# Reordering the head of a fused DeltaNet and SwiGLU kernel: chunk 1's gate/value products ahead of chunk 0's outputs, weight conversions in pairs, the first M turned by TensorE

## The chip, the cores and the metric

One Trainium2 chip, one core of it. The metric is the device time of one launch in microseconds (us), the median of several executions. The core's engines are TensorE (PE in the profile, with its weight loads as PEld), VectorE (DVE), ScalarE (ACT), GpSimd (POOL) and SyncE (SP, which here only issues transfers). They run their own programs and wait for one another at semaphores. In the profiles a record is one logged operation; a float32 product leaves two on TensorE here. The granted clock is the share of TensorE's full clock (1.00) that was let through. "Issue" marks a wait whose cause the profile doesn't show.

## The reference

The reference draws the three weight matrices as float64, and the kernel gets them as 64-bit words.

```python
# q, k, v: (4, 8, 768, 48); beta: (4, 8, 768); w_gate, w_val: (384, 1536); w_out: (1536, 384)
k_n = k / (np.linalg.norm(k, axis=-1, keepdims=True) + 1e-06)
for t in range(S):                       # the delta rule, one (48, 48) state per head
    kt, vt, bt = (k_n[:, :, t], v[:, :, t], beta[:, :, t, None])
    y[:, :, t] = np.einsum('bhd,bhde->bhe', q[:, :, t], state)
    v_old = np.einsum('bhde,bhd->bhe', state, kt)
    state = state + bt[:, :, :, None] * np.einsum('bhd,bhe->bhde', kt, vt - v_old)
x = y.transpose(0, 2, 1, 3).reshape(B * S, H * D)        # 3072 tokens of 384
g = x @ w_gate
return ((g / (1 + np.exp(-g))) * (x @ w_val)) @ w_out
```

The kernel cuts the sequence into 12 chunks of 64 steps (256 tokens each). A chunk needs the inverse of a triangular matrix per head; two chunks share one inversion, which is done by substitution in blocks of 32 on VectorE and then joined by small products on TensorE. Three sets of products of a chunk's recurrence follow (`p_u`, `p_s`, `p_y`), and their result `x_ffn` goes through the SwiGLU part: 6 groups of gate and value products, then 2 sets of output products.

Names in the profiles: `p_...` are TensorE's results, before another engine copies them out. `kn` are the normalized keys, `kt` and `qt` the transposed keys and queries, `p_g` their Gram products (all pairs within a chunk), `a_sb` the copied Gram matrix, M the scaled blocks of it that substitution inverts, `zt` the inverse (its buffer first stages weights), `uu` the copied `p_u`, `h_f` silu(gate) times value. To turn a matrix is to transpose it.

## The kernel before

The weights arrive as float64 and are made into float32 on the chip, in 30 pieces: 18 of 512 columns for gate and value, 12 of 384 for the output weights. VectorE takes the words apart in five steps and ScalarE rebuilds the exponent between the first and the fourth:

```python
def convert(*ns):
    ...
    # VectorE: power <- words & 0x7FF00000; ScalarE: power <- rebias(power)
    # VectorE: mant  <- words & 0xFFFFF | 1<<20
    # VectorE: mant  <- low word * 2**-32 + mant
    # VectorE: power <- sign | power
    # VectorE: dst   <- mant * 2**-20 * power
    for n in ns:
        stage(n + DEPTH)          # four staging places, one transfer each
```

The pieces stand between the groups of chunk 0. The pace holds back: eight output pieces are left for the last groups. Then come chunk 0's outputs:

```python
def fill(c, at):
    if c == 0 and todo:
        n = len(filled)
        filled.append(n)
        due = len(pieces) - len(todo)
        upto = min((n // 4 + 2) * 2 * KT, N_WO)
        for _ in range(max(-(-(upto - due) // (4 - n % 4)), n // 8)):
            converts(1)
        while n == FT - 1 and todo:
            converts(2)
...
def ffn(c, point, fill):
    for f in range(0, FT, 2):
        point(c)                  # a step of the next chunk's recurrence or preparation
        ...                       # gate products, silu, value products, h_f, with fill(...)
    for bp in range(NB):
        point(c)
        ...                       # 12 output products, copy, store
...
gram(0, False); gram(1, False, "py")
turned(0, True); turned(1, True)
for _ in invert(0):               # turn M (VectorE), scale, 31 substitution steps, turn back
    pass
gram(0, True)
one = join(0, slice(0, 1))
...                               # join and recurrence of chunk 0, one piece beside each step
for c in range(NCH):
    ffn(c, point, fill)
    ...
```

Of the kernel before, what the change touches and what calls it, by code (L numbers as in the profile page):

```python
# [21 lines left out]
def kernel(  # L22
# [120 lines left out]
    DEPTH = 4  # L143
    staged = {}
    wo_flat = wo_sb.bitcast(U32).rearrange("p t d -> p (t d)")
    zt_flat = ztp[1].bitcast(U32).rearrange("p c h i -> p (c h i)")
    N_WO = len(pieces) - FT * (DM // m_wo)

    def stage(n):
        if n >= len(pieces):  # L150
            return
        _, src, t, f0, m = pieces[n]
        if n < N_WO:
            place = wo_flat[:, n % DEPTH * 2 * PIECE :][:, 0 : 2 * m]
        elif n % DEPTH < 2:
            place = zt_flat[:, n % DEPTH * 2 * PIECE :][:, 0 : 2 * m]
        else:
            tag = ("mb", "zb")[n % DEPTH - 2]
            place = work.tile([128, 2 * PIECE], U32, name="staged", tag=tag, bufs=1)
            place = place[:, 0 : 2 * m]  # L160
        staged[n] = place.rearrange("p (f two) -> p f two", two=2)
        nc.sync.dma_start(
            out=place, in_=src[t * 128 : (t + 1) * 128, f0 : f0 + m].bitcast(U32)
        )

    def convert(*ns):

        work_of = []
        for n in ns:
            dst, _, t, f0, m = pieces[n]  # L170
            words = staged.pop(n)
            mant, power = (
                ffn_pool.tile([128, PIECE], U32, name=name, tag="sil", bufs=4)[:, 0:m]
                for name in ("mant", "power")
            )
            work_of.append((dst[:, t, f0 : f0 + m], words, mant, power))
        for _, words, _, power in work_of:
            nc.vector.tensor_scalar(  # L178
                out=power,
                in0=words[:, :, 1],  # L180
                scalar1=0x7FF00000,
                scalar2=None,
                op0=ALU.bitwise_and,
            )

            nc.scalar.activation(  # L186
                power.bitcast(I32), power, ACTF.Relu, bias=rebias, scale=8.0
            )
        for _, words, mant, _ in work_of:
            nc.vector.tensor_scalar(  # L190
                out=mant,
# [6 lines left out]
        for _, words, mant, _ in work_of:  # L198
            nc.vector.scalar_tensor_tensor(  # L199
                out=mant.bitcast(FP32),  # L200
                in0=words[:, :, 0],
                scalar=2.0**-32,
                in1=mant,
# [3 lines left out]
        for _, words, _, power in work_of:  # L207
# [8 lines left out]
        for dst, _, mant, power in work_of:  # L216
            nc.vector.scalar_tensor_tensor(  # L217
                out=dst,
                in0=mant.bitcast(FP32),
# [5 lines left out]
        for n in ns:  # L225
            stage(n + DEPTH)
# [10 lines left out]

    mask_k = const.tile([128, C], FP32, name="mask_k")
    mask_q = const.tile([128, C], FP32, name="mask_q")
    for m in (mask_k, mask_q):  # L240
        nc.gpsimd.memset(m, 1.0)
        for b in range(2):
            rows = m[64 * b : 64 * b + 64]
            nc.gpsimd.affine_select(
                out=rows,
                in_=rows,
                compare_op=ALU.is_ge,
                fill=0.0,
                base=-1,
                pattern=[[1, C]],  # L250
                channel_multiplier=-1,
            )
    for b in range(2):
        nc.gpsimd.memset(mask_k[64 * b : 64 * b + R, R:C], 0.0)
        nc.gpsimd.memset(mask_k[64 * b + R : 64 * b + C, 0:R], -1.0)
# [71 lines left out]

    def turned(c, of_q, tag=None):

        x = qpad[c % QB] if of_q else knp[c % AHEAD]  # L330
        xt = work.tile([128, NB, NJ, 2, C], FP32, name="qt" if of_q else "kt", bufs=AHEAD)
        (qt if of_q else kt)[c] = xt
        p_t = ps_pair("p_t", tag or ("py" if of_q else "px")).rearrange("p bp (j n) -> p bp j n", j=NJ)
        for bp in range(NB):
            for j in range(NJ):
                nc.tensor.transpose(p_t[:, bp, j], x[:, bp, 2 * j : 2 * j + 2], ident)  # L336
        nc.scalar.copy(xt.rearrange("p bp j b i -> p bp j (b i)"), p_t)  # L337
# [3 lines left out]
    def gram(c, of_q, tag=None):  # L341

        xt = (qt if of_q else kt)[c]
        p_g = ps_pair("p_g", tag or ("py" if of_q else "px")).rearrange("p par (bp j i) -> p par bp j i", bp=NB, j=NJ)
        for bp, j, par, b, _ in every():
            nc.tensor.matmul(  # L346
                p_g[half_of(b if of_q else b ^ par), par, bp, j],
# [3 lines left out]
        if of_q:  # L351
            p_sb[c] = work.tile([128, 2, NB, NJ, C], FP32, name="p_sb", bufs=AHEAD)
            dst = p_sb[c].rearrange("p par bp j i -> p (par bp j) i")
        else:
            g = c // 2
            if c % 2 == 0:
                a_sb[g] = work.tile([128, 2, HH, C], FP32, name="a_sb")
            dst = a_sb[g][:, c % 2]
        nc.vector.tensor_tensor(  # L359
            out=dst,  # L360
            in0=p_g.rearrange("p par bp j i -> p (par bp j) i"),
            in1=(mask_q if of_q else mask_k)[:, None, :].to_broadcast([128, HH, C]),
            op=ALU.mult,
        )
# [12 lines left out]
    def invert(g):  # L377
# [9 lines left out]
        a_v = a_sb[g].rearrange("p c h i -> p i (c h)")  # L387
        z_v = ztp[g % ZB].rearrange("p c h i -> p i (c h)")
        yield from turn(
            lambda rows, half: mb[rows].rearrange("p j i -> p i j"),  # L390
# [418 lines left out]
```

## Time and profile before

| | before |
|---|---|
| device time, median of 4 runs beside the changed kernel | 816.22 us (813.55 to 816.87) |
| profiled span | 816.2 us |
| TensorE, VectorE, ScalarE, GpSimd busy | 88%, 53%, 18%, 10% |
| start to first gate product | 83.4 us, VectorE busy 66.3 |
| first gate product to end of conversions | 75.0 us, VectorE busy 69.8 |
| end of conversions to end of chunk 1's outputs | 76.6 us, TensorE busy 75.1 |
| hand-over to chunk 2 | 17.8 us |
| chunks 2 to 11 | 563.4 us, TensorE busy 559.2 |

The averages mislead: 559 of TensorE's 720 busy us lie in the last stage. The first 252.8 us are called the head below. The lines behind this table stand in the prediction.

### The profile page before, as it was taken

What the parts mean: (1) busy time and instruction counts of PE and PEld (TensorE: products, weight loads), DVE (VectorE), ACT (ScalarE), POOL (GpSimd) and SP (SyncE); (2) the same over time, 40 slices, a digit from 0 to 9 for tenths busy, and PEclk for the clock granted to TensorE, in tenths of its full rate; (3) what the DMA queues carried; (4) which work ended last, traced back from release to release, by engine and by line L of the source; (5) the groups of instructions that cost most, each with busy time, mean ns of one, the idle gap of its engine ahead of it and who ended that gap; (6) DMA issues with size and microseconds to landing.
All of it is one profiled execution on the core that took longest, in us unless ns stands there. A gap on an engine that the chain in (4) does not pass through costs nothing.

```text
span 816.2 us, 20536 instructions
## 1 busy us (share of the span) xinstructions
PE 719.5 (88%) x9384; PEld 573.6 (70%) x9384; DVE 430.8 (53%) x768; ACT 145.0 (18%) x230; POOL 80.5 (10%) x73
## 2 busy tenths in 40 slices
PE   3304868399989999999999999999999999999997
PEld 2303757268758877868868868868868778688784
DVE  3899799849824785207881157852277511011010
ACT  2003223311012111121201211211202111021110
POOL 6000032122003020030110121100000000000000
PEclk9655899599998999999999999999999999999999
DMA  8604564412013120120210211001001000000000
GB/s 192 110 1 105 174 174 110 132 31 50 0 25 58 22 49 12 22 49 15 44 23 12 40 31 31 2 21 22 2 20 22 2 21 2 10 12 1 19 1 19
DMA packets 85094, 34.45 MB, mean 42 GB/s; under 512 B 78064, under 2 KB 81136, under 8 KB 85008
## 3 DMA queue, kind: packets, MB, share of 16 engines
q1 hardware_dynamic: 79008, 27.93, 14.9%
q10 hardware_dynamic: 6000, 5.21, 2.7%
q8 instruction: 73, 1.20, 0.6%
q14 instruction: 13, 0.11, 0.0%
HBM read 28.41 MB, written 4.72 MB: 41 GB/s over the span
## 4 chain that ended last, share of the span: by engine, by line
PE 77%; DVE 15%; issue 4%; DMA 2%; POOL 1%; ACT 1%; ACTq 0%; POOLq 0%; DVEq 0%
PE p_gate L574 22%; PE p_o L595 21%; PE p_val L574 21%; PE p_g L346 2%; PE p_t L336 2%; DVE mant L199 2%; DVE power L208 2%; DVE zb L410 1%; DVE tmp L404 1%; PE p_u L505 1%; PE p_y L535 1%; DVE mant L190 1%; PE p_s L522 1%; PE p_r L484 1%; PE p_y L493 1%
## 5 line engine op out<-in xcount | busy, mean ns | idle before, releaser
L574 PE MATMUL p_gate<-x_ffn,wg_sb 128*128 128x256 f32 x864 | 205.7, 388 | 0.0
L574 PE MATMUL p_val<-x_ffn,wv_sb 128*128 128x256 f32 x864 | 198.7, 379 | 0.5 <-DVE wv_sb L217 0.5
L595 PE MATMUL p_o<-wo_sb,h_f 128*128 128x384 f32 x576 | 191.1, 490 | 0.0
L574 PEld LDWEIGHTS p_val<-x_ffn,wv_sb 128*128 128x128 f32 x864 | 164.0, 190 | 23.4 <-DVE wv_sb L217 1.2
L574 PEld LDWEIGHTS p_gate<-x_ffn,wg_sb 128*128 128x128 f32 x864 | 161.6, 192 | 23.6 <-DVE wg_sb L217 0.5
L587 DVE TENSOR_TENSOR h_f<-sil,p_val 128x512 f32<-128x512 f32 x72 | 49.3, 685 | 226.7 <-PE p_val L574 226.6
L595 PEld LDWEIGHTS p_o<-wo_sb,h_f 128*128 128x128 f32 x576 | 108.9, 191 | 72.7 <-issue 0.9
L583 ACT ACTIVATE sil<-p_gate 128x512 f32<-128x512 f32 x72 | 43.0, 597 | 211.2 <-PE p_gate L574 192.0
L410 DVE TENSOR_TENSOR zb<-zb,tmp 128x31 f32<-128x31 f32 (+15 forms) x186 | 68.5, 368 | 6.4
L404 DVE TENSOR_TENSOR tmp<-zb,mb 128x31 f32<-128x31 f32 (+15 forms) x186 | 67.8, 364 | 5.0
L314 POOL TENSOR_TENSOR norm<-norm,half 128x16 f32<-128x16 f32 x12 | 35.4, 2953 | 165.4 <-DVE norm L308 163.6
L603 ACT COPY o_sb<-p_o 128x384 f32<-128x384 f32 x24 | 11.5, 480 | 202.7 <-PE p_o L595 202.7
L318 POOL TENSOR_TENSOR kn<-kin,norm 128x768 f32<-128x768 f32 x10 | 14.8, 1479 | 293.6 <-DVE norm L317 246.6
L359 DVE TENSOR_TENSOR a_sb<-p_g,mask_k 128x1024 f32<-128x1024 f32 x12 | 14.7, 1223 | 45.2 <-PE p_g L346 45.2
L346 PE MATMUL p_g<-kt 64*64 64x64 f32 x768 | 16.1, 244 | 19.1 <-ACT kt L337 19.1
L446 PE MATMUL p_j<-zt,a_sb 32*32 32x32 f32 x768 | 8.3, 197 | 26.2 <-DVE zt L369 26.2
L346 PEld LDWEIGHTS p_g<-kt 64*64 64x64 f32 x768 | 14.5, 156 | 23.2 <-ACT kt L337 19.6
L186 ACT ACTIVATE power<-power,rebias 128x512 int32<-128x512 uint32 (+1 forms) x30 | 19.9, 677 | 58.4 <-DVE power L178 56.2
L446 PEld LDWEIGHTS p_j<-zt,a_sb 32*32 32x32 f32 x768 | 7.5, 108 | 28.8 <-issue 28.7
L372 DVE STREAM_TRANSPOSE zt<-zb 32x1024 f32<-32x1024 f32 x12 | 26.3, 2188 | 0.1
L372 DVE STREAM_TRANSPOSE mb<-a_sb 32x1024 f32<-32x1024 f32 x12 | 25.6, 2136 | 0.3
L465 DVE COPY zt<-p_j 32x1024 f32<-32x1024 f32 (+1 forms) x7 | 7.5, 1070 | 32.3 <-ACT zt L465 32.2
(85 smaller groups left out, 548.1 us busy)
## 6 DMA issues: line engine op xcount, KB each, us to landing
wo_sb<-in_moe_w_gate_dram SPq DMA_DIRECT2D x9, 512.0 KB, 3.6
wo_sb<-in_moe_w_val_dram SPq DMA_DIRECT2D x9, 512.0 KB, 3.8
qpad<-in_q_dram SPq DMA_DIRECT2D x48, 96.0 KB, 3.0
vin<-in_v_dram SPq DMA_DIRECT2D x96, 48.0 KB, 2.4
out_dram<-o_sb ACTq DMA_DIRECT2D x48, 96.0 KB, 2.2
kin<-in_k_dram SPq DMA_DIRECT2D x44, 96.0 KB, 2.9
staged<-in_moe_w_out_dram SPq DMA_DIRECT2D x6, 384.0 KB, 3.2
zt<-in_moe_w_out_dram SPq DMA_DIRECT2D x6, 384.0 KB, 3.6
```

What stands on the lines that cost most here:

```text
L186: nc.scalar.activation(power.bitcast(I32), power, ACTF.Relu, bias=rebias, scale=8.0)
L199: nc.vector.scalar_tensor_tensor(out=mant.bitcast(FP32), in0=words[:, :, 0], scalar=2.0**-32, in1=mant, op0=ALU.mult, op1=ALU.add,)
L208: nc.vector.scalar_tensor_tensor(out=power, in0=words[:, :, 1], scalar=0x80000000, in1=power, op0=ALU.bitwise_and, op1=ALU.bitwise_or,)
L314: nc.gpsimd.tensor_tensor(out=norm, in0=norm, in1=half, op=ALU.pow)
L346: nc.tensor.matmul(p_g[half_of(b if of_q else b ^ par), par, bp, j], kt[c][half_of(par), bp, j, b], xt[half_of(par), bp, j, b],)
L372: nc.vector.transpose(out(rows, 0), in_(rows, 0))
L404: nc.vector.tensor_tensor(out=t_v, in0=zb[:, 0 : j + 1, j : j + 1].to_broadcast([128, j + 1, m]), in1=mb[:, j : j + 1, j + 1 : R].to_broad ...
L410: nc.vector.tensor_tensor(out=zb[:, 0 : j + 1, j + 1 : R], in0=zb[:, 0 : j + 1, j + 1 : R], in1=t_v, op=ALU.add,)
L574: nc.tensor.matmul(ps[name][:, i], w_sb[:, t, (f + i) * 128 : (f + i + 1) * 128], x[:, t], start=(t == 0), stop=(t == KT - 1),)
L583: nc.scalar.activation(sil, ps[name], ACTF.Silu)
L587: nc.vector.tensor_tensor(out=hs[-1][:, f % 4 : f % 4 + 2], in0=sil, in1=ps["p_val"], op=ALU.mult)
L595: nc.tensor.matmul(p_o, hs[f // 4][:, f % 4, bp * 128 : (bp + 1) * 128], wo_sb[:, f], start=(f == 0), stop=(f == FT - 1),)
```

## The change

Its intent is to let TensorE work through the conversions: chunk 1's gate/value products need no output weights, so four of chunk 1's six groups go ahead of chunk 0's outputs. VectorE's chain is shortened: pieces go in pairs (a step of one hides the latency of the other's), the exponent is asked for a pair ahead, eight pieces are staged early, and the first M is turned by 128 small products instead of three VectorE transposes. The diff, cut to its core:

```diff
 def convert(ns, ahead=2):
     ...                                  # pairs; mantissas are built in dst itself
+        for n in range(ns[-1] + 1, ns[-1] + 1 + ahead):
+            power_step(n)                # exponents of the next pair
     ...
 def fill(n):
     if todo:
+        converts(2 - len(filled) % 2)    # 2, 1, 2, 1, ...
+        filled.append(n)
-        ...                              # the old pace
+def invert_first(g, between):
+    for j in range(R):
+        for quad, at in QUADS:
+            nc.tensor.matmul(
+                p_m[quad, R * j : R * j + R], a_v[quad, :, at + j], ident[quad, quad])
+    between(0)                           # four exponents, two pieces
+    scale_m(mb, p_m.rearrange("p (j i) -> p j i", i=R), nbeta)
+    between(1)                           # query transposes and Gram products
+    for _ in substitute(mb, zb):
+        pass
+    ...
+def join_first(g, c, tags):
+    # first set: 32 products 32x32, two ScalarE copies; second set: 32 of 32x64, two copies
 ...
-        for c in range(NCH):
-            ffn(c, point, fill)
+        second = join_first(0, 1, ("px", "py"))       # chunk 1's join: before the first group
+        for f in range(0, FT, 2):
+            point(1)
+            gate_val(0, f, fill)
+        finish(1)
+        for f in range(0, FT, 2):
+            if f == 8:
+                while todo:
+                    converts(2)
+                for bp in range(NB):
+                    point(2)
+                    output(0, bp, fill)
+            point(2)
+            gate_val(1, f, fill)
+        for bp in range(NB):
+            point(2)
+            output(1, bp, fill)
```

## The prediction

> **What bounds the kernel now.** I read three views. First, the busy time per engine, cut at five moments that I chose after looking at the timeline: the first gate product (83.4), the end of the weight conversions (158.4), the end of chunk 1's outputs (235.0), the first gate product of chunk 2 (252.8), the end.
>
> ```profile
> core 0: us, PE busy (x) PEld busy (x) DVE busy (x) ACT busy (x) POOL busy (x), PEclk, DMA share, GB/s
> 0.00:83.40 83.40, 24.90 (x775) 22.05 (x775) 66.26 (x123) 14.73 (x24) 13.96 (x28) 0.68 0.48 108
> 83.40:158.40 75.00, 48.16 (x613) 40.69 (x612) 69.76 (x137) 23.86 (x38) 11.52 (x6) 0.82 0.52 152
> 158.40:235.00 76.60, 75.06 (x736) 56.37 (x732) 52.28 (x91) 9.46 (x14) 12.54 (x9) 0.97 0.12 25
> 235.00:252.80 17.80, 12.16 (x472) 11.27 (x472) 4.42 (x6) 5.37 (x8) 5.08 (x3) 0.81 0.25 48
> 252.80:816.20 563.40, 559.17 (x6806) 443.25 (x6805) 238.07 (x412) 91.62 (x147) 37.43 (x29) 1.00 0.10 20
> ```
>
> From 252.8 on TensorE is busy 559.2 of 563.4 us at full clock: only less TensorE work would shorten that part, and the change removes none there. The head, 252.8 us, is the target. Up to 158.4 VectorE is the bound (66.3 of 83.4 us, then 69.8 of 75.0); TensorE idles 58.5 + 26.8 us there. From 158.4 to 235 TensorE is full again.
>
> Second, TensorE's timeline where the two bounds meet, and the hand-over to chunk 2:
>
> ```profile
> 134.32 2.75 PE L574 MATMUL p_val<-x_ffn,wv_sb 128*128 128x256 f32 x12
> 136.91 1.04 PE L336 MATMUL p_t<-ident,kn 128*128 128x128 f32 x8
> 137.78 1.04 PE L336 MATMUL p_t<-ident,qpad 128*128 128x128 f32 x8
> 156.84 1.99 PE L346 MATMUL p_g<-kt 64*64 64x64 f32 x64 [18.02 <-ACT kt L337]
> 158.60 1.93 PE L346 MATMUL p_g<-qt,kt 64*64 64x64 f32 x64
> 160.46 9.17 PE L595 MATMUL p_o<-wo_sb,h_f 128*128 128x384 f32 x24
> ```
>
> Chunk 0's gate/value products end at 137, but TensorE stands still for 18.0 us until ScalarE has copied kt. That copy stands in ScalarE's program behind the exponent steps of the last eight pieces, which wait for VectorE. In truth this is a wait for the output weights: chunk 0's outputs come next and need all 30 pieces. Chunk 1's products, which need none of the output weights, only begin at 182.
>
> Third, VectorE's timeline, for the price of a piece. A lone gate piece, then a pair of output pieces:
>
> ```profile
> 119.72 0.69 DVE L217 SCALAR_TENSOR_TENSOR wg_sb<-mant,power 128x512 f32<-128x512 f32 x1
> 120.33 0.42 DVE L178 TENSOR_SCALAR power<-wo_sb 128x512 uint32<-128x512 uint32 x1
> 120.66 0.42 DVE L190 TENSOR_SCALAR mant<-wo_sb 128x512 uint32<-128x512 uint32 x1
> 121.12 0.69 DVE L199 SCALAR_TENSOR_TENSOR mant<-wo_sb,mant 128x512 f32<-128x512 uint32 x1
> 121.73 0.68 DVE L208 SCALAR_TENSOR_TENSOR power<-wo_sb,power 128x512 uint32<-128x512 uint32 x1
> 122.44 0.69 DVE L217 SCALAR_TENSOR_TENSOR wv_sb<-mant,power 128x512 f32<-128x512 f32 x1
> ...
> 142.72 0.62 DVE L178 TENSOR_SCALAR power<-staged 128x384 uint32<-128x384 uint32 x2
> ...
> 146.61 0.62 DVE L178 TENSOR_SCALAR power<-zt 128x384 uint32<-128x384 uint32 x2
> ```
>
> Starts are what counts: 120.33 to 123.05 (the next piece) is 2.72 us for a lone piece of 512, with starts 0.33, 0.46, 0.61, 0.71, 0.61 apart. The steps that need the one just before (0.46, 0.71) lose 0.10 to 0.13. A pair has other work in between: 142.72 to 146.61 is 3.89 us for two pieces of 384, or 1.95 each. For a pair of 512 I estimate 2 x (0.33 + 0.33 + 3 x 0.61) = 4.98.
>
> **What the skill says.** "TensorE: Matmul & The Clock Gate", section What's actually happening: the array's clock is halved until TensorE has been busy for some 3.4 us. The trace agrees: the granted clock was 0.50 from 40 to 60 us, and the first twelve gate products took 5.01 us against 2.75 to 2.86 later. "GPSIMD Engine Reference", section Specifications: GpSimd shares its memory interfaces with VectorE instructions that take two inputs or use both ports. It shows: while GpSimd scaled a kn (109.35 to 110.87) and squared the next, two conversion steps took 1.69 and 1.83 instead of 0.42 and 0.69. "Perfetto Trace Analysis", section Optimization Strategy, advises interleaving regimes with different bounds: that is this change.
>
> **The change, part by part.** The program order of every engine can be read from the built kernels, so I walked the head by hand with durations of this trace.
>
> 1. Start to the first gate product. Norm 1 now stands behind norm 0's power step (2.93 us on GpSimd): kn of chunk 1 comes at 18.3, not 17.2. The second Gram matrix ends at 24.0 and goes out through ScalarE (two copies, about 1.1). The three VectorE transposes (24.26 to 30.70, 6.4 us) go; instead 128 small products, 256 records. Those of beta took 1.50 us for 96, so 4.0. Scaling M starts at 29.3 instead of 30.8: only 1.5 gained on the path, but VectorE uses the wait for four exponent masks and two pieces (5.7 us). Substitution is unchanged (23.4 us), ending at 53.9. Then one full transpose (2.2) and one into d_t (2.1) replace three (6.4) and the six of z1 (2.3), and the mask of p_g leaves the path: first join products at 56.1, two ScalarE copies of 0.57, second products about 1.4, two copies of 1.0: p_u at 61.9, against 68.9. Of these 7.0 us I give back about 4: uu, y and x_ffn stand on ScalarE behind exponent steps of pieces 4 to 10, which VectorE reaches only at 64 to 77; and the second half of the join stands before the first gate product. Gate product: about 80 instead of 83.4, with nine pieces done or nearly so instead of six.
>
> 2. Conversions. From 78 on: pieces 9, 10 (5.0), then idle until the slow-clock value product at 87.6 for h_f (4.4 lost). After h_f, at 88.3: pieces 11 to 17 (3 lone x 2.72 + 2 pairs x 4.98 = 18.1), 18 to 28 (3 lone x 2.1 + 4 pairs x 3.9 = 21.9), five more h_f (0.6 each, 3.0), two masks, two reductions, r, state, small norm steps (about 5.7), GpSimd collisions (twice 2.4): 53.5 in all, to 141.8. Then h_f of chunk 1's first group and piece 29: 144.4. Staging output weights goes round four places only, and the exponent wants its words a pair ahead, with some 2.7 us between the freeing and the need, against 3.2 to 3.6 from issue to landing: 2 to 3 us more. End at 146.5 instead of 158.4: 11.9 gained.
>
> 3. What TensorE has left then. Before: two p_g, four outputs, six groups, five more products and transposes, 76.6. After: chunk 0's six groups and chunk 1's first are done; its second ends near 149.5, and four groups (5.2 each, 20.8), four outputs (4 x 7.8 = 31.2) and four small ones (about 3.7) follow: outputs end at 205.2, 58.7 after the conversions. 17.9 gained. VectorE's second inversion begins when chunk 3's Gram matrix is out (about 158) and is spread over the same groups. Its last steps come behind h_f of the last group (190): nine substitution steps 5.2, three transposes 6.5, z1 2.3: 204. It just fits.
>
> 4. Hand-over to chunk 2: 17.8 before. One join product set (1.3) and its copy (0.6) no longer lie beside the last output, so 19.4: 1.6 lost. First gate product of chunk 2: 224.6 instead of 252.8, 28.2 earlier.
>
> 5. The rest. From there both orders agree row by row, but the query side is done just in time: two chunks' query transposes and Gram products (0.87 + 1.01 each) move from the head into the full part: 3.8 lost.
>
> Sum: 11.9 + 17.9 - 1.6 - 3.8 = 24.4; 815.7 - 24.4 = 791.3. Say 791.
>
> **Rivals.** (a) VectorE and TensorE wait for each other in chunk 0's groups: each h_f stands between a pair and a lone piece, h_f waits for TensorE, TensorE for PSUM or for uu behind exponent steps (5.7 us before, 5.3 in my walk). I found one VectorE wait of 4.4; for it speaks the shorter order with three pieces per group from the first, against it that VectorE needs about 8 us per group and TensorE about 6.5. If there were three such waits: some 8 us lost, 799. (b) The second inversion ends the head: it fits by 1 us in my walk. Every GpSimd collision or late Gram copy goes straight into the hand-over; 5 to 8 us, 797 to 799. (c) The output weights' transfers end the conversions: before, DMA ran at about half its time here without stalling VectorE, but the exponents now need words earlier. One us per piece would be 10: 801. (d) Better than I think: the Gram copies in halves and the deeper early staging bring VectorE's idle to nothing and ScalarE's queue is short: 783.
>
> **Range and chances.** The tail (563 us) is safe to within 2 us, so all doubt is in the head. Two rivals at half strength give 799, the good case 783. Range 783 to 800. Two per cent is 799.4: faster 0.87, within 2% 0.12, slower 0.01.
>
> **What would show it.** In the changed profile: p_m of 256 records in about 4 us; no 18 us wait for kt; last conversion near 146; outputs of chunk 0 after four of chunk 1's groups; first gate product of chunk 2 near 225; from there about 567 us, nearly full. Wrong if VectorE idles over 8 us between 60 and 147, if the second inversion ends over 3 us after the outputs, or if the full part has grown by more than 5 us.

## The result, and the profile after

The changed kernel takes 804.78 us (median of 4 runs, 802.04 to 806.05) against 816.22 for the one before. The ratio is 0.9861, with a 95% interval of 0.9827 to 0.9896: 1.4% faster, within the 2% that count as the same. The prediction of 791 (783 to 800) was wrong.

The first view of the changed kernel is the busy time per engine between the same five moments as in the prediction (columns: window, length, then us and instructions per engine, the granted TensorE clock, the DMA share and GB/s):

```profile
0.00:87.76 87.76, 37.24 (x1031) 33.53 (x1031) 64.42 (x139) 22.25 (x38) 14.02 (x23) 0.68 0.61 154
87.76:154.95 67.19, 57.15 (x708) 49.15 (x708) 57.02 (x113) 21.94 (x37) 12.13 (x6) 0.86 0.39 103
154.95:215.27 60.32, 60.32 (x358) 43.53 (x356) 49.12 (x93) 6.57 (x12) 11.83 (x8) 1.00 0.08 17
215.27:234.88 19.61, 13.65 (x599) 12.57 (x599) 4.51 (x7) 6.01 (x10) 3.39 (x3) 0.83 0.18 35
234.88:802.80 567.92, 563.69 (x6952) 446.98 (x6950) 241.38 (x430) 94.69 (x164) 39.11 (x29) 1.00 0.11 22
```

Set against the rows of before, stage by stage (all of the profiled span; the predicted column is the prediction's moments, and its last entry 816.2 - 24.4 - 224.6):

| stage | before | predicted | after | after minus predicted |
|---|---|---|---|---|
| start to first gate product | 83.4 | 80 | 87.8 | +7.8 |
| to end of conversions | 75.0 | 66.5 | 67.2 | +0.7 |
| to end of chunk 1's outputs | 76.6 | 58.7 | 60.3 | +1.6 |
| hand-over to chunk 2 | 17.8 | 19.4 | 19.6 | +0.2 |
| chunks 2 to 11 | 563.4 | 567.2 | 567.9 | +0.7 |

The middle of the head is shorter by 24.1 us (75.0 + 76.6 against 67.2 + 60.3), nearly as predicted (26.4). In it TensorE idles 10.0 us (127.5 less 57.15 and 60.32) where it idled 28.4 before. But the first gate product, which was to come 3.4 us earlier, comes 4.4 later, and that is most of the miss of 11.

The second view is TensorE's timeline of the changed kernel up to that product (start, length, engine, operation, operands, in brackets the idle time before it and what ended it):

```profile
26.42 1.78 PE L457 MATMUL p_m<-ident,a_sb 32*32 32x32 f32 x109 [1.21 <-ACT a_sb L392]
30.12 2.04 PE L457 MATMUL p_m<-ident,a_sb 32*32 32x32 f32 x128 [1.92 <-issue]
34.12 0.55 PE L457 MATMUL p_m<-ident,a_sb 32*32 32x32 f32 x19 [1.97 <-issue]
...
61.63 1.92 PE L487 MATMUL p_j<-zt,a_sb 32*32 32x32 f32 x64 [22.00 <-DVE zt L465]
64.28 0.39 PE L496 MATMUL p_j<-t_first,d_t 32*32 32x64 f32 x2 [0.73 <-issue]
64.94 3.59 PE L496 MATMUL p_j<-t_first,d_t 32*32 32x64 f32 x62 [0.27 <-ACT t_first L490]
70.68 1.96 PE L599 MATMUL p_u<-vin,zt 64*64 64x48 f32 x64 [2.15 <-ACT zt L499]
...
87.76 5.49 PE L665 MATMUL p_gate<-x_ffn,wg_sb 128*128 128x256 f32 x12
```

Look at the counts of the first three rows: 109, 128, 19. The turn of M is 256 records of some 17 ns, 4.4 us of work; but TensorE stands twice for 1.9 us, for nothing that the profile can name ("issue"), and the two waits are exactly 128 records apart. So the turn ends at 34.7, not 29.1. The 128 products have two records each, and the profile counts as many weight loads as product records (9640 of both): 128 records are 256 instructions. The profile's table of queues lists 75 transfers of instructions with 1.23 MB in all on one queue, 16.4 KB each; the 19,280 instructions in blocks of 256 make about 75. The Trainium skill, "Runtime: NRT & Kernel Launch", section Instruction fetch mechanics, says that an engine's instructions come in blocks of 16 KiB, 256 instructions, and that the cost of a block boundary is mostly hidden. The count agrees to the record; the hiding doesn't: a block lasts TensorE 2.04 us here, and the next came 4.0 us after the one before (30.12 to 34.12), while the core's DMA engines were 0.91 busy (mean of 25 to 35 us). The kept trace also holds the times of these transfers. Two of them landed at 28.62 and 32.55, and TensorE went on 1.50 and 1.57 us later. In all 17 kernels that turn M on TensorE, the run of records after the second wait starts 1.27 to 1.57 us after such a landing.

The lower rows: the first join set takes 1.92 us and the second, of 64 records, 0.39 + 3.59, where 1.4 had been predicted; the first gate set takes 5.49, twice its later 2.75.

The third view is VectorE's waits in the changed kernel from 60 to 160 us (total, times, longest). Before, the longest such row was 3.5 us, for ScalarE's exponents.

```profile
DVE h_f L677 <- PE p_val L665: 8.7, 2, 7.5
DVE power L184 <- DMA zt<-in_moe_w_out_dram: 1.3, 1, 1.3
DVE power L184 <- DMA staged<-in_moe_w_out_dram: 0.9, 2, 0.7
DVE power L224 <- ACT power L192: 0.7, 1, 0.7
```

VectorE stands 7.5 us for the first value products: it has done all that its program puts ahead of the first `h_f`. The waits for transfers come to 2.2 us. From 60 to 147 us, the stretch that the prediction names, VectorE is busy 76.4 of 87 us.

The last view is TensorE where chunk 1's groups begin, to be held against the wait of 18.0 us of before:

```profile
149.42 1.98 PE L371 MATMUL p_g<-kt 64*64 64x64 f32 x64 [4.33 <-ACT kt L361]
...
172.56 7.91 PE L683 MATMUL p_o<-wo_sb,h_f 128*128 128x384 f32 x24
```

The wait for kt is 4.33 us now, and chunk 0's outputs begin 18 us after the last conversion, free of any wait. The join of the second inversion starts at 215.27, where the last output ends: the second inversion fits.

### The profile page after: what moved, and what is told of

Same layout as the page of the kernel before. It is cut to its first block, busy times and chain, and to the rows that moved or that the text cites. A ratio compares the mean times of both kernels' runs of the same rounds, so it can differ in the third digit from the quotient of the medians.

```text
span 802.8 us, 21132 instructions
## 1 busy us (share of the span) xinstructions
PE 732.1 (91%) x9640; PEld 585.8 (73%) x9640; DVE 416.4 (52%) x778; ACT 151.5 (19%) x260; POOL 80.5 (10%) x68
## 3 DMA queue, kind: packets, MB, share of 16 engines
q8 instruction: 75, 1.23, 0.6%
## 4 chain that ended last, share of the span: by engine, by line
PE 81%; DVE 6%; DMA 2%; issue 1%; ACT 1%; DVEq 0%
PE p_o L683 23%; PE p_gate L665 23%; PE p_val L665 21%; PE p_g L371 3%; PE p_t L359 2%; PE p_r L578 1%; PE p_u L599 1%; PE p_y L587 1%; PE p_y L629 1%; PE p_s L616 1%; DVE power L224 1%; PE p_f L650 1%; DVE power L184 1%; DMA staged<-in_moe_w_out_dram 1%; PE p_j L555 1%
## 5 line engine op out<-in xcount | busy, mean ns | idle before, releaser
L392 DVE COPY a_sb<-p_g 128x512 f32<-128x512 f32 x22 | 14.1, 685 | 32.7 <-PE p_g L371 32.7
L487 PE MATMUL p_j<-zt,a_sb 32*32 32x32 f32 x128 | 3.8, 237 | 22.0 <-DVE zt L465 22.0
L595 DVE TENSOR_TENSOR vin<-vin,p_r 128x768 f32<-128x768 f32 x11 | 10.5, 954 | 25.3 <-PE p_r L578 25.0
L405 DVE STREAM_TRANSPOSE zt<-zb 32x1024 f32<-32x1024 f32 x10 | 22.0, 2196 | 0.1
L405 DVE STREAM_TRANSPOSE mb<-a_sb 32x1024 f32<-32x1024 f32 x10 | 21.3, 2133 | 0.3
L559 DVE COPY zt<-p_j 32x1024 f32<-32x1024 f32 x5 | 6.1, 1222 | 27.4 <-ACT zt L559 27.4
L359 PE MATMUL p_t<-ident,kn 128*128 128x128 f32 x96 | 14.3, 298 | 6.5 <-DVE kn L329 6.5
```

The costliest lines, as they stand in the source:

```text
L359: nc.tensor.transpose(p_t[bp][:, at], x[:, bp, 2 * j : 2 * j + 2], ident)
L405: nc.vector.transpose(out(rows, 0), in_(rows, 0))
```

## The experiments

Eighteen kernels ran, all correct. Each is told against the kernel before of the same rounds; the changed kernel's ratio to keep in mind is 0.9861. The first twelve asked where the expected gain had gone, the last six whether the late first gate product carries the miss.

### 1. Four pieces' transfers issued later (x_late)

```diff
-        for n in range(4, EARLY):
-            stage(n)                     # right behind load_v(0)
 ...
     def between(n):
         ...
+            for m in range(4, EARLY):
+                stage(m)                 # behind the turn of M
```

> The changed kernel, with the four extra early weight loads (pieces 4 to 7, 2 MB) put behind the turning of M instead of before it. In the changed profile the 256 small products that turn M took from 26.4 to 34.7 us, with two waits named issue of 1.9 us, 128 products apart. Theory A (TensorE runs through small products faster than its instructions arrive, one block of 128 products per 3.7 to 4 us): the two waits stay, the turn still takes about 8.2 us, and the total stays within 2 us of 804.8. Theory B (the early loads hold the instructions up): the waits go, the turn takes about 4 us, scaling M starts near 31 instead of 34.8, and the total falls by 3 to 4 us.

(The expectation calls records products: the turn is 128 products, 256 records.) It took 802.51 us (2 runs) against 815.7, ratio 0.9831 (0.9802 to 0.986). The rows of the turn in its timeline:

```profile
25.13 1.79 PE L457 MATMUL p_m<-ident,a_sb 32*32 32x32 f32 x109 [1.20 <-ACT a_sb L392]
27.32 2.01 PE L457 MATMUL p_m<-ident,a_sb 32*32 32x32 f32 x128 [0.41 <-issue]
31.33 0.55 PE L457 MATMUL p_m<-ident,a_sb 32*32 32x32 f32 x19 [1.99 <-issue]
```

The turn starts 1.3 us earlier and lasts 6.75 us instead of 8.25; the first gate product comes at 84.97. One wait shrank from 1.92 to 0.41, the other stayed: from 25 to 35 us the DMA engines were 0.54 busy instead of 0.91, so the weights' transfers cost something here, but the last block, again 4.0 us after the one before (27.32 to 31.33), came no sooner for it.

### 2. M turned by VectorE again (x_dveturn)

```diff
-        for j in range(R):
-            for quad, at in QUADS:
-                nc.tensor.matmul(p_m[...], a_v[quad, :, at + j], ident[quad, quad])
-        between(0)
-        scale_m(mb, p_m..., nbeta)
+        for _ in turn(mb, a_t):          # three VectorE transposes, as before
+            pass
+        scale_m(mb, mb, nbeta)
```

`between(0)`, with its two pieces, moves behind the substitution.

> The changed kernel, with M turned by VectorE again (three transposes); the four exponent masks and the two conversions that stood beside TensorE's turn now stand after the mask of the first query Gram matrix. Theory A (TensorE's turn takes 8.2 us and gains nothing over VectorE's 6.4): M is scaled by about 34 instead of 36, substitution ends about 2 us earlier, the two pieces (5.7 us) mostly fill VectorE's idle 7.5 us before the first h_f: 802 to 807 us. The prediction's step (TensorE's turn gains 1.5 us on the path and 5.7 us of VectorE): 810 to 812.

808.40 us against 815.7, ratio 0.9905 (0.9878 to 0.9931). The first join set starts at 60.47, 1.2 us earlier than with TensorE's turn; but the two pieces that had lain beside the turn now stand beside the join: the copy between the join sets comes on ScalarE behind four exponents of 2.56 us in all, TensorE waits 3.81 us there, and the first gate product comes at 91.39, 3.6 later. So against this placement of the two pieces the turn by TensorE gains about 3.6 us, and not by ending sooner: by freeing VectorE for pieces. The intervals of the two ratios overlap, 808.4 lies between the two expectations, and no run put the pieces into VectorE's 7.5 us of idle time instead.

### 3. Chunk 0's outputs first again (x_noorder)

```diff
+        while todo:
+            converts(2)
+        for bp in range(NB):
+            point(1)
+            output(0, bp, fill)
         finish(1)
         for f in range(0, FT, 2):
-            if f == 8:
-                ...                      # outputs of chunk 0 here
             point(2)
             gate_val(1, f, fill)
```

> The changed kernel, with chunk 0's outputs again before chunk 1's gate/value products, all pieces converted before them. If the order is what gains (it took TensorE's work after the conversions from 76.6 to 60.3 us): 818 to 823 us, and TensorE stands still for some 15 us again before chunk 0's outputs. If most of the gain came from cheaper conversions: 805 to 809.

805.53 us against 815.7, ratio 0.9864 (0.9845 to 0.9883): the same as with the new order. The outputs start at 138.94 beside the last pieces and wait 5.9 us in three waits for single pieces; conversions end at 154.1 and chunk 1's outputs at 215.9, against 154.95 and 215.27. The order, the heart of the change, gains nothing measurable here.

### 4. Pieces one at a time, no exponent ahead (x_single)

```diff
-            convert(todo[:n], ahead)
-            del todo[:n]
+            for _ in range(n):
+                convert(todo[:1], 0)
+                del todo[:1]
```

> The changed kernel, with each piece converted alone and its exponent taken in its own turn, none ahead. Nine or ten pairs fewer at about 0.45 us each: conversions end 4 to 5 us later, 808 to 811 us, if VectorE is the bound up to there. If transfers or TensorE set that time, 804 to 806. With exponents not wanted ahead, VectorE's waits for transfers of output weights (2.2 us in the changed kernel) should go.

806.2 us against 815.7, ratio 0.9875 (0.9853 to 0.9896). VectorE waits 9.8 us for ScalarE's exponents instead of 0.7, 7.6 of them at once, and not at all for transfers or the first value products. Pairs and exponents ahead are worth about 1.4 us by the medians, which the intervals don't tell from nothing: most of the time they save had another wait behind it.

### 5. The kernel before, without the step ahead of its first output (b_nopoint)

```diff
         for bp in range(NB):
-            point(c)
+            if c > 0 or bp > 0:
+                point(c)
```

In the kernel before, this step holds the Gram products that waited 18.0 us for kt.

> The kernel before, with one line changed: the piece of recurrence work that stood ahead of chunk 0's first output (transposes and Gram products of chunk 2, whose ScalarE copy waited behind the exponents of the last eight pieces) is left out there and comes at the next point. Theory A (the 18 us idle of TensorE is a wait for the output weights, met half way: a product of outputs can follow the pieces as they are converted): the first output set streams beside the last conversions and is over about 1 us after them, the total falls by about 8 us to 807 to 809. Theory B (all of the output weights are needed before anything of use can run): within 2 us of 815.7.

812.64 us against 816.89, ratio 0.9961 (0.9929 to 0.9993). Three rows of its timeline:

```profile
139.44 0.91 PE L596 MATMUL p_o<-wo_sb,h_f 128*128 128x384 f32 x2 [0.33 <-DVE wo_sb L217]
142.23 0.91 PE L596 MATMUL p_o<-wo_sb,h_f 128*128 128x384 f32 x2 [1.88 <-DVE wo_sb L217]
145.65 2.93 PE L596 MATMUL p_o<-wo_sb,h_f 128*128 128x384 f32 x4 [2.51 <-DVE wo_sb L217]
```

With the 18 us wait gone, the outputs start 23 us earlier than in the kernel before and wait for output weights piece by piece. Of 18 us, 3 to 4 are gained: the rest was indeed a wait for output weights, as the prediction had read it. (The profile is of the slowest of the four runs, 816.21 us.)

### 6 to 8. VectorE's idle time filled, and idle products on TensorE (y_fill, y_warm, y_both)

```diff
 # y_fill
                 converts(2)
+                converts(1)              # a third piece beside the turn of M
 ...
+            if not filled:
+                converts(2)              # three more pieces ahead of the first h_f
+                converts(1)
 # y_warm, behind the query transposes in between(1)
+                for _ in range(20):
+                    nc.tensor.matmul(keep, ident, wg_sb[:, 0, 0:512])
 # y_both: these two and the later transfers of x_late
```

> The changed kernel, with four more pieces converted where VectorE stands idle: one beside TensorE's turn of M (idle 4.3 us there) and three before the first h_f (idle 7.5 us). If VectorE's idle time before the first h_f is what the late first gate product cost: conversions end at 144 to 147 instead of 155, and the total falls by 7 to 10 us, to 795 to 798. If TensorE is the bound from the first gate product on, 802 to 805.

803.55 us against 816.89, ratio 0.9846 (0.9825 to 0.9868). The 7.5 us wait shrank to 1.7, but 4.3 us of waiting for ScalarE's exponents (now behind the silu) and 3.1 for a transfer took its place. Conversions end at 151.3 instead of 154.95, chunk 1's outputs at 213.3 instead of 215.3.

> The changed kernel, with 20 products of no use (512 columns, the result never read) on TensorE while VectorE substitutes, so that the granted clock is up when the join begins. Theory A (the join's small products are slow because the clock is halved): the second join set takes 2.1 to 2.4 us instead of 4.3, the first gate set 2.9 instead of 5.5, the first gate set starts 4 to 6 us earlier, total 797 to 801. Theory B (they are slow because only two of the four row groups are in use or because instructions arrive late): join sets as before, the total within 2 us of 804.8.

802.05 us, ratio 0.9821 (0.9799 to 0.9844). The idle products ended at 55.7, 5.1 us ahead of the join, and the join sets were as slow as before (1.92 and 3.59): this run didn't test the clock. All the same its profiled span is 2.5 us shorter than the changed kernel's (800.3 against 802.8), of which 0.9 lie ahead of the first gate product: there the turn ended 1.0 us sooner. The end of the turn scatters by 1.4 us (from 33.3 in z_gap to 34.7) among kernels whose TensorE programs agree up to there.

> The changed kernel with both edits, and with the four early loads behind the turn of M as in x_late. If the idle before the first h_f is one and the same loss, the gains don't add: conversions end at 142 to 145, total 791 to 796. If they were independent, 785 to 789.

803.38 us, ratio 0.9845 (0.9815 to 0.9874). The parts don't add; but here the idle products ended 7.7 us ahead of the join, so the clock was not tested either.

### 9. Old order and old pace together (x_noorder_pace)

```diff
 # as x_noorder, and in fill:
-            converts(2 - len(filled) % 2)
+            k = len(filled)
+            due = len(pieces) - len(todo)
+            upto = min((k // 4 + 2) * 2 * KT, N_WO)
+            for _ in range(max(-(-(upto - due) // (4 - k % 4)), k // 8)):
+                converts(1)
```

> x_noorder (outputs of chunk 0 first again) with the old pace of conversions as well: one or two per call in chunk 0's groups, the last eight held back for the outputs. Theory A (the order of the products and the pace of the conversions are two ways to the same gain: with three pieces per group only three are left when chunk 0's groups end, so outputs first lose nothing): 811 to 816 us, nearly all the gain of the change gone. Theory B (the order gains nothing and the pace neither; the gain comes from fewer VectorE steps in the head): 804 to 808.

814.93 us against 817.52, ratio 0.9968 (0.9951 to 0.9986). Here nearly the whole gain is gone. TensorE's waits in this kernel (total, times, longest), and one of them in its timeline:

```profile
PE p_o L683 <- DVE wo_sb L233: 10.9, 5, 3.8
```

```profile
144.13 2.92 PE L683 MATMUL p_o<-wo_sb,h_f 128*128 128x384 f32 x4 [3.77 <-DVE wo_sb L233]
```

The first set of outputs crawls from 136.09 to 161.6, where TensorE needs 7.9 us for it. What the order protects against is exactly this: output products ahead of output weights. The new pace protects against it too, by having the weights ready.

### 10 to 12. More idle products; a step moved; all together (z_warm, z_mid, z_best)

```diff
 # z_warm
+                for _ in range(24):      # y_warm had 20
+                    nc.tensor.matmul(keep, ident, wg_sb[:, 0, 0:512])
 # z_mid: the recurrence step between a group's silu and its conversions
                 nc.scalar.activation(sil, ps[name], ACTF.Silu)
+                then()                   # point(1), which stood ahead of the group
                 fill(2)
 # z_best: x_late, 22 idle products, z_mid, and six pieces moved to VectorE's idle times
```

> y_warm again with 24 products of no use instead of 20, so that at most 2 us lie between the last of them and the join (in y_warm TensorE stood still for 5.1 us there and the join ran exactly as slowly as before). Theory A (clock): second join set 2.1 to 2.4 us instead of 4.3, first gate set 2.9 to 3.5 instead of 5.4, first gate set starts at 81 to 84 instead of 86.9 to 87.8; total 797 to 800. Theory B (two row groups, or instructions late): join sets stay at 1.9 and 4.3 us, total 801 to 805.

799.80 us (799.21 to 801.57) against 817.52, ratio 0.9781 (0.9765 to 0.9798): the fastest of all, and 2.2% faster than the kernel before. The join in its timeline:

```profile
61.44 1.20 PE L487 MATMUL p_j<-zt,a_sb 32*32 32x32 f32 x64 [2.11 <-DVE zt L465]
63.36 0.29 PE L496 MATMUL p_j<-t_first,d_t 32*32 32x64 f32 x2 [0.72 <-issue]
64.02 3.38 PE L496 MATMUL p_j<-t_first,d_t 32*32 32x64 f32 x62 [0.37 <-ACT t_first L490]
```

The first set takes 1.20 us instead of 1.92. The second and the first gate set (5.30) stay slow. In the profiles 3.2 us lie between this kernel and the changed one: 1.1 up to the first gate product, 0.8 from there to the end of the outputs, 1.2 in the hand-over; the medians differ by 5.0. The join (start of its first set to `p_u`) is 0.9 us shorter. But y_warm, without a faster join, already had 2.5 of the 3.2: most of the gain isn't by the clock at the join, and that the idle products cause it isn't shown.

> The changed kernel, with each recurrence step of chunk 0's groups placed between a group's silu and its conversions instead of ahead of the group: its ScalarE copy then no longer stands behind the exponents of the pieces of the group before. If TensorE's wait for uu (4.5 us) is only ScalarE's order: the wait falls under 1.5 us and the total by 2 to 4 us, 800 to 803. If VectorE is the bound there anyway: the wait moves elsewhere, 803 to 806.

807.06 us, ratio 0.987 (0.9854 to 0.9885). The wait only moved: VectorE stood 9.6 us for the query Gram products.

> All that helped: early loads behind the turn of M, a warm clock at the join, one more piece beside the turn of M, five pieces around the join's second half with their exponents ahead of the copies, recurrence steps in the middle of a group. If the head is bound by VectorE up to the end of the conversions and these fill its idle 12 us: conversions end near 142, total 790 to 795. If each gain is taken back by the next wait, as in y_both: 800 to 804.

800.69 us, ratio 0.9796 (0.9774 to 0.9819). This is the most telling of the misses: conversions end at 144.6, earlier than even the prediction had them, and chunk 1's outputs at 212.57, 68.0 us later. In the changed kernel these are 154.95 and 60.3. Its two stages, from the first gate product on:

```profile
86.42:144.60 58.18, 47.66 (x667) 40.74 (x670) 53.19 (x106) 19.50 (x33) 13.82 (x7) 0.91 0.37 99
144.60:212.57 67.97, 67.97 (x408) 50.12 (x401) 48.71 (x94) 7.17 (x13) 10.09 (x7) 0.98 0.07 16
```

VectorE is done ten microseconds sooner and the outputs end 2.7 sooner: TensorE idles 10.5 us in the two stages together, as much as in the changed kernel (10.0). The run holds several edits, z_mid's too, which alone gained nothing, so this isn't a clean test of VectorE's time. y_fill, with one edit, has conversions end 3.7 us sooner and outputs 2.0.

### 13 to 16. The start of the gate products, the clock, and the fourth corner (z_jl, z_gap, z_jlgap, x_pace)

```diff
 # z_jl: chunk 1's join and query Gram products behind the first group, not ahead of it
         for f in range(0, FT, 2):
-            point(1)
+            if f == 2:
+                while first:
+                    first.pop(0)()
+            elif f > 2:
+                point(1)
             gate_val(0, f, fill)
 # z_gap: z_warm, and between the two join sets of chunk 0
+            for _ in range(5):
+                nc.tensor.matmul(pair[:, 1], ident, wg_sb[:, 0, 0:512])
 # z_jlgap: z_jl, z_gap and x_late
 # x_pace: the changed kernel with the old pace in fill (as in x_noorder_pace)
```

> The changed kernel with the second half of the join (two sets of 64 small products, 1.92 and about 3.6 us, and their copies) moved from ahead of chunk 0's first gate/value group to behind it. Same work. Theory A (the late first gate product carries the miss; from it on TensorE's own chain of work and waits is the bound): the first gate product at about 81 instead of 87.8, but the moved sets stay on TensorE behind it, so only the waits around them go: 798 to 802. Theory B (VectorE's conversions or the output pieces end the head whatever TensorE starts with): conversions end within 1 us of 155, total 803.5 to 805.5. Theory C (chunk 1's recurrence, which needs the join, starts later and holds up chunk 1's products): slower than the changed kernel, 806 or more.

805.77 us against 815.84, ratio 0.9881 (0.9859 to 0.9904). The first gate product comes 7.2 us earlier, and the total is no shorter. A row of TensorE's and one of VectorE's timeline tell why:

```profile
80.54 5.12 PE L665 MATMUL p_gate<-x_ffn,wg_sb 128*128 128x256 f32 x12 [0.89 <-ACT x_ffn L651]
```

```profile
100.11 1.29 DVE L384 TENSOR_TENSOR p_sb<-p_g,mask_q 128x512 f32<-128x512 f32 x2 [8.35 <-PE p_g L371]
```

The join with its two copies now stands between the first and the second group, and VectorE stands 8.35 us for what comes behind it. The chain was moved, not shortened.

> The changed kernel with 24 idle products of 512 columns ahead of the join and 5 more directly behind the first join set, while ScalarE copies it. Theory clock: the second set's 64 products fall from about 3.6 us to 2.0 to 2.5, the first gate product comes at about 85.3, total 798 to 799.5. Theory of the products' own form (two row groups, 64 columns): the second set stays at 3.3 us or more at a granted clock that is no longer halved, and the total stays at the 799.8 of 24 idle products alone, or 1 us above it.

805.65 us, ratio 0.9877 (0.9851 to 0.9903). The join in its timeline:

```profile
60.33 1.20 PE L488 MATMUL p_j<-zt,a_sb 32*32 32x32 f32 x64 [2.11 <-DVE zt L465]
...
66.74 0.29 PE L500 MATMUL p_j<-t_first,d_t 32*32 32x64 f32 x2 [0.72 <-issue]
67.39 1.99 PE L500 MATMUL p_j<-t_first,d_t 32*32 32x64 f32 x62 [0.37 <-ACT t_first L494]
```

The second set's 62 records take 1.99 us instead of 3.59, at a granted clock of 1.00 instead of 0.50: here the clock was the cause. The form of the products counts as well. The first join set of the kernel before, also 64 records:

```profile
57.74 1.08 PE L446 MATMUL p_j<-zt,a_sb 32*32 32x32 f32 x64 [26.20 <-DVE zt L369]
```

It took 1.08 us at a granted clock of 0.50, where the changed kernel's first set took 1.92 at 0.50 and 1.20 at 1.00. The old set wrote all four blocks of 32 partitions, the new one writes two of them; no run tests that difference alone.

The warm clock doesn't pay: the five idle products last 4.56 us and the second set had to queue behind them, so `p_u` comes at 71.54 against 69.55 in z_warm.

> The changed kernel with the second half of the join behind the first group, pieces 4 to 7 issued later, 24 idle products ahead of the join and 5 between its two sets. If the gains of these add: 804.8 - 2.3 (late issue) - 5 (idle products) - 4 (join moved) = 793 to 796. If TensorE's own chain from the first gate product on is the bound and the start comes at about 78: 795 to 798. If conversions or VectorE bind: 799 to 801, as the run that filled VectorE's idle time did.

803.6 us, ratio 0.9856 (0.9834 to 0.9878): it missed all three expectations. The first gate product came at 80.62.

> The changed kernel, with chunk 1's groups ahead of chunk 0's outputs, but with the old pace of conversions (eight output pieces held back and spread over the groups). If order and pace are two ways to the same gain, each enough by itself: 804 to 807, as the changed kernel. If the pace is what gains and the order does nothing: 811 to 815, as old order with old pace (814.9).

803.12 us, ratio 0.9857 (0.9837 to 0.9877). This fills the table of order and pace, everything else as in the changed kernel:

| ratio to the kernel before | old pace | new pace |
|---|---|---|
| chunk 0's outputs first | 0.9968 | 0.9864 |
| chunk 1's groups first | 0.9857 | 0.9861 |

Either of the two gives the whole gain of about one per cent; the second adds nothing to it.

### 17 and 18. The join cut up between the groups (z_inter, z_interwarm)

```diff
 # z_inter
         for f in range(0, FT, 2):
-            point(1)
+            if 0 < f < 6:
+                first.pop(0)()           # one set of the join
+            elif f == 6:
+                first.pop(0)()           # query Gram products
+                point(1)
+            elif f > 6:
+                point(1)
             gate_val(0, f, fill)
 # z_interwarm: the same with 24 idle products and the later transfers
```

> The changed kernel with the second half of the join cut up: its first set behind chunk 0's first group, its second set behind the second group, the query Gram products behind the third; chunk 1's recurrence one or two steps later. Theory A (the late start carries the miss): first gate product at about 80.5 instead of 87.8, no wait of VectorE over 4 us in the groups, total 797 to 800. Theory B (TensorE's work and VectorE's conversions bind and the start does not matter): 803 to 806. Theory C (chunk 1's recurrence comes too late, and TensorE stands before chunk 1's first group): a wait of 3 us or more there, total 801 to 804.

804.79 us against 815.27, ratio 0.9863 (0.9847 to 0.988). The first gate product comes at 80.45, where the prediction had it. Two later rows of TensorE's timeline:

```profile
109.40 2.06 PE L587 MATMUL p_y<-state,qt 64*64 64x48 f32 x64 [5.45 <-DVE p_sb L384]
...
143.62 1.97 PE L359 MATMUL p_t<-ident,qpad 128*128 128x128 f32 x8 [7.66 <-ACT x_ffn L651]
```

Chunk 1's recurrence is later, its results stand in VectorE's and ScalarE's queues behind conversions, and TensorE waits 5.45 and 7.66 us there. In the changed kernel its two large waits in this stretch were 4.50 (for uu) and 4.33 (for kt). Chunk 2's first gate product is at 234.88, as in the changed kernel to the hundredth.

> As the run before, with 24 idle products ahead of the join and pieces 4 to 7 issued later. If the gains add: 5 us less than the run before for the idle products, 1 to 2 for the later issue: 791 to 795 under theory A, 797 to 800 under B, 795 to 799 under C.

800.84 us, ratio 0.9821 (0.9802 to 0.984), some 4 us less than z_inter. Two edits are in it, the idle products and the later transfers, and the run doesn't part them. The first gate product comes at 77.88, ahead of the predicted 80, and yet the total is no better than z_warm's.

## Why the prediction was wrong

**Step 1 failed.** It put the first gate product at about 80 because the 128 products of the turn were to take 4.0 us, by analogy with beta's 96 records in 1.50, and the second join set 1.4. The first size took a small product's own time and left out what comes between. The turn took 8.25: 4.4 of work, about as assumed, and 3.9 of two waits 128 records apart, the length of a block of instructions, each ending 1.5 to 1.6 us after a block had landed. Beta's 96 records are shorter than a block. The kernel before has such waits too, 128 records (40 + 64 + 24) apart at its hand-over:

```profile
238.43 0.80 PE L484 MATMUL p_r<-state,kt 64*64 64x48 f32 x40 [1.61 <-issue]
239.89 1.15 PE L493 MATMUL p_y<-state,qt 64*64 64x48 f32 x64 [0.66 <-DVE zt L465]
240.88 0.56 PE L505 MATMUL p_u<-vin,zt 64*64 64x48 f32 x24
242.16 0.80 PE L505 MATMUL p_u<-vin,zt 64*64 64x48 f32 x40 [0.72 <-issue]
```

The turn also began at 26.4, not 25.1. So M was scaled at 34.8, 5.5 us later than predicted, and the substitution and the first join set carry the same 5.5. The join adds 3.3 (`p_u` at 70.68 against 61.9, 8.8 late): its first set took 1.92 (the sum leaves it about 1.3; the kernel before had needed 1.08), and the second with its wait 4.25 instead of 1.4. By z_gap a full clock would have made them 1.20 and 2.65, so the halved clock is most of that; but the clock was halved in the kernel before as well (1.08 at 0.50), and what was new is the form of the products. 1.0 was won back up to the gate product: 7.8 late.

**Step 2 was right from its start on.** Conversions took 67.2 us where 66.5 were predicted. VectorE's idle time ahead of the first `h_f` was 7.5 instead of 4.4, because its pieces were done sooner; the first `h_f` itself came 8.3 us after the first gate product, where 7.6 had been predicted. Transfers cost 2.2 us, within the predicted 2 to 3. The GpSimd collisions came as well: while GpSimd scaled a kn and squared the next (111.14 to 114.27), two steps took 1.70 and 1.95 us instead of 0.42 and 0.69, as by the shared interfaces that the prediction cites, and a second collision followed at 138.8.

**Step 3 had the size right (60.3 against 58.7) and its reason incomplete.** It read the 18.0 us wait rightly as one for output weights (b_nopoint), but took the new order for the only cure. The table of order and pace shows that the new pace alone cures it too, since it brings the output weights earlier. And the step hung the end of the outputs on the end of the conversions. z_best speaks against that: conversions 10 us earlier, outputs 2.7. From the first gate product on, the changed kernel's TensorE idles only 10.0 of 127.5 us, so little was left there for a gain on VectorE to win.

**Steps 4 and 5** held: 19.6 against 19.4, and 4.5 us lost in the rest against 3.8. Of the rivals, (a) was partly there, with one long wait and not three. The sign that the prediction gave for being wrong, VectorE idle for over 8 us between 60 and 147, came true: it idled 10.6 us, 7.5 of them for the first value products. (b) and (c) weren't there: the second inversion's join followed the last output at once, and the waits for transfers stayed within step 2's allowance.

**What stays open.** The sum by stages puts 7.8 of the 11 us on the late first gate product. That a start at 80 would have brought the predicted total isn't shown, and four runs speak against it: z_jl, z_inter, z_jlgap and z_interwarm started at 77.9 to 80.6 and took 805.8, 804.8, 803.6 and 800.8. All had to put the second half of the join elsewhere, where it made new waits. No run shortened the chain ahead of the gate products by 7 us with everything else in place. The delivery of instructions as the cause of the two waits rests on the count of 128 records, the size and the landing times of the instruction transfers, and x_late, where the transfers landed at 25.81 and 29.77 and TensorE went on 1.51 and 1.56 us later; no run changed the number of products.

## What to carry to other kernels

Two parts of a change can be two cures for one wait; try each alone before counting both gains. When an engine is moved off a chain, many tiny products aren't priced by their duration: look at where their instructions come from, at the clock that they run at, and at the queue behind which their result is copied. And where one engine is nearly full through a stage, as TensorE here with 10 us of idle time in 127, a gain on another engine there buys little: in z_best ten us on VectorE came with 2.7 at the end of the outputs.

## What the Trainium skill lacked or had wrong

- "Runtime: NRT & Kernel Launch", section Instruction fetch mechanics, calls crossing a block of instructions mostly hidden. With small products it wasn't: 2.04 us of work per block of 256 instructions, then 1.92 and 1.97 us of waiting, with one block every 4.0 us (0.41 and 1.99 with fewer transfers under way), and work going on 1.5 to 1.6 us after a block had landed. The page gives no rate at which blocks arrive.
- "TensorE: Matmul & The Clock Gate", section Why this matters for your kernels, says to leave no idle gap over about 3 us. In z_warm no gap between the idle products and the gate products was over 2.2 us, and yet the clock was halved again by the second join set; in the changed kernel the clock stayed at 0.50 from 60 to 93 us while the records of small products covered 9.29 of the 15 us from 60 to 75 and 9.53 of the 12.7 up to 87.7. So the advice wasn't enough here. The page's section A second HAM failure mode: psum-queue depth-cycling does say that frequent short idle times between groups of products can throttle the clock again, which this trace agrees with; but no section says how much of a window small products must fill to count as busy.
- "Perfetto Trace Analysis", section Optimization Strategy, advises interleaving regimes. It doesn't say that the order on the waiting engine and the pace on the busy one can be substitutes: 0.9857, 0.9864 and both together 0.9861.
